# Queue positions and unit orders in a saturated spectral and SwiGLU block

## The chip, the cores and the metric

The kernel runs on one core of a Trainium2 chip. The metric is the device time of one execution in microseconds (us). The engines are TensorE (PE, with its weight loads PEld), VectorE (DVE), ScalarE (ACT), GpSimd (POOL) and SyncE (SP); each works through its own queue of instructions, and they meet through semaphores.

## The reference

One block with adaptive layer norms, all in fp32, for 2048 rows of width 512, inner width 1792:

```
mod = (silu(c) @ w_mod)            -> sa, ca, ga, sb, cb, gb
h = layernorm(x) * (1 + ca) + sa
a, b = h @ dft_hid_re.T, h @ dft_hid_im.T
x = x + ga * (dft_seq_re @ a - dft_seq_im @ b)
h = layernorm(x) * (1 + cb) + sb
x = x + gb * ((silu(h @ w1) * (h @ w3)) @ w2)
```

## The kernel before

Every fp32 operand is split into a high part, rounded to the multiplier's format (ACT, line 87, `copy`), and a low part, the rest (DVE, line 90, `minus`). A product is three matmuls: high by high, low by high, high by low. Sums of two tiles are `plus` (DVE, line 93), elementwise products `times` (DVE, line 96). Large tiles live in slots that are taken and given back in program order; the eight PSUM banks are named by number.

The first part is a layer norm and the transform along the width, until 85 us. Its products use line 576, and its last rows end in bank 5; `ho` (line 93) combines that bank with an earlier copy of it.

Then come 32 units of the transform along the sequence (`seq_unit`, line 750), until about 263 us. It accumulates eight sums, x0 to x3 and y0 to y3, in the eight banks: `x` e in bank 2e and `y` e in bank 2e + 1, so that y2 has bank 5. Each unit adds four matmuls to each x and two to each y. The first unit runs while the last rows of the transform before are still in bank 5: `between()`, the None in its order, issues those last products after x0 and x1.

The last part is the gated layer. A few plain blocks come first; then the work is twelve `items`, numbered from 0, each a group of 256 inner columns for one pair of the four tiles of 512 rows. Items 0 to 4 belong to pair 0, items 5 to 11 to pair 1; item 5 is `turning`. In an item the two large products are made from seven factors each, `a1` to `a7` for w1 and `b1` to `b7` for w3 (`factor`); each is six matmuls and accumulates in a bank that is copied out on the way (`x`, ACT line 87). The downs, `y`, multiply by w2: in items 5 to 9 again by seven factors (`seven_unit`), elsewhere directly (`down_unit`). Their results are copied out as `y` by ACT at line 335 and added to memory by a DMA that POOL issues; the last two groups' results are added by DVE instead (line 1146).

The order on PE is written out by hand as a string of units for each item, `head + body`. A minus sign marks a factor of the item before: an item's last three factors, b7, b4 and b3, run in the next item's head. A `y` takes the next of the queued downs, `seconds`.

What the other engines do for a unit is queued in program order too. `delayed()` runs at the start of each unit, and `behind(n, fn)` makes `fn` run n units later; so the number sets where an instruction stands in the queue of ACT or DVE. `result` and `seven_parts` queue the high and the low part of the gated product `hf` in this way. `beside` fills what remains of each unit with splits of weights and other background work from `jobs`: w1, w2 and w3 have a high `w1h`, a low `w1l`, and the same of their sums (`w1s`, four operations on DVE; `w1sh`, `w1sl`). `th` and `tl` are parts of the sums of the layer's input.

`judge` adds up what a check has gathered in `chk` and sets `bad`; a branch after the last down reads it.

Of the kernel before, what the change touches and what calls it, by code (L numbers as in the profile page):

```python
# [42 lines left out]
def folded(nc, pools, c, cp, wmr, wmc, x, xt, ctr, cti, wdr, wdi, w1, w3, w2, out):  # L43
# [22 lines left out]
    def give(t):  # L66
        slot, _ = slot_of.pop(id(t))
        free.append(slot)
# [657 lines left out]
    def seq_unit(n, m, between=None):  # L726
        j, k = steps[n]
        l, d, high = lo.pop((n, m)), df.pop((n, m)), bh[n][:, m, :]
        begin, turn, end = (k, m) == (0, 0), (k, m) == (NK // 2 - 1, 1), (k, m) == (NK - 1, 1)
        if begin:  # L730
            for e in range(ND):
                acc["x", e], acc["y", e] = bank(2 * e), bank(2 * e + 1)

        def own(t, e):
            return flat(t[k])[:, m * N + e * P : m * N + (e + 1) * P]

        def run(what, e):
            if what == "x":
                terms = [
                    (own(us, e), high),  # L740
                    (own(ul, e), high),
                    (own(us, e), l[:, 0, :]),
                    (own(uh, e), l[:, 1, :]),
                ]
                if k == NK // 2 and m == 1:
                    terms.append((zz[:97, 0, cols(e)], zz[:97, 1, :]))
            else:
                terms = [(own(us, e), d[:, 0, :]), (own(uh, e), d[:, 1, :])]
            for i, (lhs, rhs) in enumerate(terms):
                nc.tensor.matmul(  # L750
                    acc[what, e],
                    lhs,
                    rhs,
                    start=begin and i == 0,
                    stop=(end or (turn and what == "x")) and i == len(terms) - 1,
                    skip_group_check=what == "x" and k >= NK // 2,
                )


        order = [(what, e) for what in "xy" for e in range(ND)]  # L760
        if (k, m) == (NK // 2, 0):
            order = order[ND:] + order[:ND]
        if between:
            order = [(what, e) for e in range(ND) for what in "xy"]
            order = order[0:1] + order[2:3] + [None] + order[1:2] + order[3:]
        for at in order:
            if at is None:
                between()
            else:
                run(*at)  # L770
        give(l)
        give(d)
        if m == 1:
            give(bh.pop(n))
            if j == 1:
                for t in (uh, us, ul):
                    give(t.pop(k))

        if turn:
            for e in range(ND):  # L780
                residual(j + 2, e, acc["x", e], ga2)
        if end:
            part = [take(F32, "sum") for _ in range(2)]
            for e in range(ND):
                copy(part[e // 2][:, e % 2, :], acc["x", e])
                residual(j + 2, e, acc["y", e], ga)
            for i in range(2):
                for t in (j, j + 2):
                    step(background, 0, lambda i=i, t=t: add_sums(t, i, part[i]), 1.3)
                step(background, 0, lambda i=i: give(part[i]))  # L790
# [448 lines left out]
    def result(i, w, q, k, src):  # L1239

        g, pair = items[i]
        v = vs[i][q][:, k, :]
        if w == "w1":
            behind(k != 0 or q == 0, lambda: nc.scalar.activation(v, src, AF.Silu))  # L1244
            return
        times(v, v, src)
        if (g, pair) in SEVEN:
            seven_parts(i, q, k)
            return

        def highs():
            hf[g, PAIRS[pair][k], q] = take(F32R, "hf")
            copy(hf[g, PAIRS[pair][k], q][:, 0, :], v)

        def lows():
            u = hf[g, PAIRS[pair][k], q]
            minus(u[:, 1, :], v, u[:, 0, :].bitcast(F32))

        behind(1, highs)
        behind(2, lows)  # L1260

    def seven_parts(i, q, k):
        key = items[i]
        v = {(a, b): vs[i][a][:, b, :] for a in range(2) for b in range(2)}

        def high(n, src):
            right7[key, n] = take(F32R, "hf")
            copy(right7[key, n][:, 0, :], src)

        def low(n, src):  # L1270
            u = right7[key, n]
            minus(u[:, 1, :], src, u[:, 0, :].bitcast(F32))

        if (q, k) != (0, 1):
            n = {(0, 0): 1, (1, 0): 2, (1, 1): 3}[q, k]
            behind(1, lambda: high(n, v[q, k]))
            behind(2, lambda: low(n, v[q, k]))
            return
        t1, t2, t3, t4 = v[0, 0], v[1, 1], v[0, 1], v[1, 0]
        behind(1, lambda: minus(t1, v[0, 1], v[0, 0]))  # L1280
        behind(2, lambda: high(5, t1))
        behind(2, lambda: minus(t3, v[1, 1], v[0, 1]))
        behind(3, lambda: low(5, t1))
        behind(3, lambda: minus(t2, v[1, 1], t1))
        behind(4, lambda: high(7, t3))
        behind(4, lambda: minus(t4, v[1, 0], t2))
        behind(5, lambda: high(6, t2))
        behind(5, lambda: low(7, t3))
        behind(6, lambda: high(4, t4))
        behind(7, lambda: low(6, t2))  # L1290
        behind(8, lambda: low(4, t4))
# [69 lines left out]
    def factor(i, w, n):  # L1361
        g, pair = items[i]
        key = (w, g, pair)
        st = state.setdefault((i, w), {})
        new = n in (1, 2, 5)
        if new:
            st[TO[n]] = bank(TO[n] + (0 if w == "w1" else 3))
        to = st[TO[n]]
        names = ("h", "l") if LEFT[n][0] == "h" else ("sh", "sl")
        for d in range(2):  # L1370
            at = slice(int(LEFT[n][1]) * HALF + d * P, int(LEFT[n][1]) * HALF + (d + 1) * P)
            product(
                to,
                [flat(wuse[key][x])[:, at] for x in names],
                [x[:, d, :] for x in right(pair, n)],
                new and d == 0,
                d == 1,
                not new,
            )
        if n == 1:  # L1380
            st["x"] = take(F32, "x")
            if w == "w1":
                vs[i] = [take(F32, "v") for _ in range(2)]
        if n == 5:
            st["y"] = take(F32, "x")
        if n in (1, 5, 6):
            copy(st["y" if n == 5 else "x"][:, n // 6, :], to)
        elif n == 4:
            result(i, w, 1, 0, to)
        else:  # L1390

            own = st["y" if n == 7 else "x"][:, n % 2 if n < 7 else 0, :]
            q, k = {2: (0, 0), 3: (0, 1), 7: (1, 1)}[n]
            dst = vs[i][q][:, k, :] if w == "w1" else own
            plus(dst, to, own)
            result(i, w, q, k, dst)
            if n == 7:
                behind(1, lambda: give(st["y"]))
        st["n"] = st.get("n", 0) + 1
        if st["n"] == 7:  # L1400
            for x in wuse.pop(key).values():
                give(x)
        if n == 3:
            behind(1, lambda: give(st["x"]))
            if w == "w3":
                for x in vs.pop(i):
                    behind(9 if items[i] in SEVEN else 3, lambda x=x: give(x))


    loads.extend((n, m) for n in range(len(steps)) for m in range(2))  # L1410
# [340 lines left out]
    def unit(kind, i, n):  # L1751
# [9 lines left out]
            drain(lambda: ("t", 1, {6: 2, 5: 1, 7: 3, 4: 4}[n]) in done, jobs)  # L1761
        delayed()
        factor(i, "w1" if kind == "a" else "w3", n)
        if (kind, i, n) == ("b", turning + 1, 4):
            judge()
        if (kind, n) == ("a", 1):
            load_w(("w1", *items[i + 1]) if more else ("w2", g, pair))
        if (kind, n) == ("a", 6):
# [30 lines left out]
    for i in range(len(items)):  # L1799
        body = "a6 a5 y y a7 y a3 y a4 y b1 y b2 y b6 b5 y"  # L1800
        if i and items[i - 1] in SEVEN:
            body = "a6 a5 a7 y a3 a4 y b1 b2 y b6 b5 y"
        spread = i > 1 and items[i - 2] in SEVEN
        if spread and i < len(items) - 1:
            body = body.replace("a6", "a6 y", 1)
# [2 lines left out]
        if i == turning:  # L1808
            body = "y y y y y a6 y a5 y a7 y b1 b2 a4 b6 a3 b5"
        if i == len(items) - 1:  # L1810
            body = "a6 a5 a7 a3 a4 b1 b2 y b6 y b5 y b7 y b4 y y b3 y y y y y y y y y y"
        head = "-b7 a1 -b4 -b3 a2 " if i == turning else "-b7 a1 a2 -b4 -b3 " if i else "a1 a2 "
        if spread and i < len(items) - 1:
            head = "-b7 a1 y a2 -b4 y -b3 "
# [1 line left out]
            head = "-b7 y a1 a2 y -b4 y -b3 "  # L1816
        for at in (head + body).split():
            if at == "y":
                if (i, len(seconds)) == (len(items) - 1, 4):
                    tc.mark_branch_hint_location("general", hint="LikelyTaken")  # L1820
                down(*seconds.popleft())
            elif at[0] == "-":
                unit(at[1], i - 1, int(at[2]))
            else:
                unit(at[0], i, int(at[1]))
# [804 lines left out]
```

## Time and profile before

| | |
|---|---|
| median of 3 runs | 696.4 us (695.23 to 697.4) |
| profiled execution | 694.86 us, of which the span 693.1 us |
| PE busy in the span | 675.3 us (97%) |
| DVE, ACT, POOL busy | 586.9, 451.1, 131.6 us |
| granted PE clock | 0.997 |

Rows of the timeline give the start and duration of an instruction, or of several like ones (x2), in us, then engine, line, operation and tiles; brackets hold the idle time of the engine before it and what ended that. Rows of the waits give the total, the number of times and the longest.

### The profile page before, as it was taken

Reading aid. Unit: us, or ns where it says so; the run is one execution under the profiler, and the core shown is the slowest. Engines: PE = TensorE matmul, PEld = TensorE weight load, DVE = VectorE, ACT = ScalarE, POOL = GpSimd, SP = SyncE. Lnnn points to the kernel's source line nnn. Section 1 sums busy time; section 2 is a strip of 40 time slices with the busy share of each in tenths; the row PEclk is TensorE's granted clock in tenths of the full one; section 3 lists DMA queues with packets and bytes.
Section 4 is the critical chain, followed back from the end, with each engine's and each line's share of the span. In section 5 each row is a group of like instructions: output and inputs, shape, how many; then the busy total and the mean of one; then the engine's idle time right before and its main releaser. Section 6 shows DMA issues by size and latency. Waiting matters only on the chain.

```text
span 693.1 us, 9032 instructions
## 1 busy us (share of the span) xinstructions
PE 675.3 (97%) x3122; PEld 558.1 (81%) x3122; DVE 586.9 (85%) x945; ACT 451.1 (65%) x751; POOL 131.6 (19%) x156
## 2 busy tenths in 40 slices
PE   7999899999999999999999999999999999999996
PEld 5899778888888888888788888887877888888785
DVE  5999759998999988889997989787999979888374
ACT  4998946545353575664577767867676988877520
POOL 1320252543435000010101001011002212221100
PEclk9999999999999999999999999999999999999999
DMA  9730289787588540173667666476849898999713
GB/s 264 222 123 1 71 306 352 259 294 253 181 310 263 181 157 30 37 148 122 102 145 147 152 154 117 96 132 121 258 89 208 152 208 168 186 214 172 179 42 126
DMA packets 40261, 116.80 MB, mean 169 GB/s; under 512 B 5136, under 2 KB 5392, under 8 KB 40208
## 3 DMA queue, kind: packets, MB, share of 16 engines
q0 software_dynamic: 14512, 50.86, 36.5%
q1 hardware_dynamic: 25264, 63.98, 27.9%
q10 hardware_dynamic: 432, 1.31, 0.5%
q8 instruction: 26, 0.43, 0.3%
q14 instruction: 27, 0.22, 0.1%
HBM read 76.81 MB, written 41.42 MB: 171 GB/s over the span
## 4 chain that ended last, share of the span: by engine, by line
PE 71%; DVE 9%; issue 7%; DMA 5%; ACT 4%; POOL 1%; SPq 1%; another core or an unknown queue 1%; POOLq 0%; ACTq 0%; DVEq 0%
PE bank L100 43%; PE bank L750 25%; DMA sum<-y 3%; POOL sum L1352 1%; PE bank L559 1%; DMA w<-in_wdr 1%; PE bank L598 1%; ACT y L335 1%; DVE v L96 1%; SPq L231 1%; DMA w<-in_wdi 1%; DVE xr L805 1%; DVE ul L90 1%; DMA x<-in_x 0%
## 5 line engine op out<-in xcount | busy, mean ns | idle before, releaser
L100 PE MATMUL bank<-hf,w2h 128*128 128x512 f32 (+1 forms) x352 | 108.5, 389 | 0.4 <-ACT y L335 0.4
L87 ACT ACTIVATE hf<-v 128x512 fp32r<-128x512 f32 x71 | 44.4, 631 | 69.1 <-DVE v L96 53.7
L335 ACT ACTIVATE y<-bank,gb 128x512 f32<-128x512 f32 x118 | 76.5, 682 | 4.1 <-PE bank L100 3.6
L100 PEld LDWEIGHTS bank<-hf,w2h 128*128 128x128 f32 x352 | 65.5, 188 | 16.1 <-ACT y L335 2.2
L1160 POOL DMA_DIRECT2D sum<-y x28 | 24.0, 857 | 240.7 <-ACT y L335 124.5
L100 PE MATMUL bank<-hf,w2l 128*128 128x512 f32 (+1 forms) x176 | 68.1, 387 | 0.0
L90 DVE TENSOR_TENSOR hf<-v,hf 128x512 fp32r<-128x512 f32 x71 | 48.7, 686 | 9.8 <-ACT hf L87 9.8
L1352 POOL DMA_DIRECT2D sum<-y x35 | 29.8, 852 | 129.4 <-ACT y L335 120.4
L750 PE MATMUL bank<-d,us 128*128 128x512 f32 x128 | 49.9, 390 | 1.5 <-DVE ho L93 1.5
L87 ACT ACTIVATE x<-bank 128x512 f32<-128x512 f32 x72 | 41.7, 591 | 13.3 <-PE bank L100 12.1
L750 PE MATMUL bank<-bh,us 128*128 128x512 f32 x128 | 49.9, 390 | 0.0
L750 PE MATMUL bank<-bh,ul 128*128 128x512 f32 x128 | 49.8, 389 | 0.0
L750 PE MATMUL bank<-d,uh 128*128 128x512 f32 x128 | 49.8, 389 | 0.0
L750 PE MATMUL bank<-l,us 128*128 128x512 f32 x128 | 49.8, 389 | 0.0
L750 PE MATMUL bank<-l,uh 128*128 128x512 f32 x128 | 49.8, 389 | 0.0
L170 POOL DMA_INDIRECT re<-in_ctr,mirror x32 | 35.1, 1095 | 64.8 <-DVE ul L90 38.5
L170 POOL DMA_INDIRECT im<-in_cti,mirror x32 | 32.9, 1029 | 38.2 <-PE bank L750 10.0
L93 DVE TENSOR_TENSOR x<-bank,x 128x512 f32<-128x512 f32 x36 | 24.7, 685 | 17.3 <-PE bank L100 17.1
L100 PEld LDWEIGHTS bank<-hf,w2l 128*128 128x128 f32 x176 | 33.1, 188 | 6.6
L1244 ACT ACTIVATE v<-v 128x512 f32<-128x512 f32 x36 | 22.7, 629 | 22.5 <-DVE v L93 22.1
L93 DVE TENSOR_TENSOR v<-bank,x 128x512 f32<-128x512 f32 x36 | 24.7, 686 | 13.4 <-PE bank L100 12.5
L100 PE MATMUL bank<-h2h,w1h 128*128 128x512 f32 x80 | 31.1, 389 | 0.0
(260 smaller groups left out, 1904.7 us busy)
## 6 DMA issues: line engine op xcount, KB each, us to landing
sum<-y POOLq DMA_DIRECT2D x63, 512.0 KB
w<-in_w SPq DMA_DIRECT2D x42, 512.0 KB
re<-in_ctr SPq DMA_DIRECT2D x32, 256.0 KB
im<-in_cti SPq DMA_DIRECT2D x32, 256.0 KB
wmc<-in_wmc SPq DMA_DIRECT2D x8, 512.0 KB
xr<-in_xt SPq DMA_DIRECT2D x8, 512.0 KB
sum<-xr SPq DMA_DIRECT2D x8, 512.0 KB
x<-in_x SPq DMA_DIRECT2D x11, 256.0 KB
```

The lines of the kernel that those rows point to most:

```text
L87: nc.scalar.activation(dst, src, AF.Copy, scale=scale)
L90: nc.vector.tensor_tensor(out=dst, in0=a, in1=b, op=OP.subtract)
L93: nc.vector.tensor_tensor(out=dst, in0=a, in1=b, op=OP.add)
L96: nc.vector.tensor_tensor(out=dst, in0=a, in1=b, op=OP.mult)
L100: nc.tensor.matmul(acc, lhs[a], rhs[b], start=first and n == 0, stop=last and n == len(PASSES) - 1, skip_group_check=more,)
L170: nc.gpsimd.indirect_dma_start(dst, None, rows, bass.IndirectOffsetOnAxis(ap=at, axis=0))
L231: queue.dma_start(raw_w[dt][q * 64 : (q + 1) * 64, m, :], w[i][par::2, q])
L335: nc.scalar.activation(dst, src, AF.Identity, scale=by)
L750: nc.tensor.matmul(acc[what, e], lhs, rhs, start=begin and i == 0, stop=(end or (turn and what == "x")) and i == len(terms) - 1, skip_grou ...
L1160: nc.gpsimd.dma_start(sums[t, d // 2], y, accum_op=OP.add)
L1244: behind(k != 0 or q == 0, lambda: nc.scalar.activation(v, src, AF.Silu))
L1352: nc.gpsimd.dma_start(sums[t, which], y, accum_op=OP.add)
```

## The change

Five things move; nothing is added or taken away.

1. The first unit of the sequence transform runs y2 last, behind x3 and y3.
2. The highs of hf are queued two units behind their unit instead of one, the lows three instead of two; so are the first three parts in `seven_parts`, and v is given back one unit later outside SEVEN.
3. `judge` moves from item 6 (after b4) into the last item, ahead of the second of its last ten downs.
4. Item 6 (`turning + 1`) has its own body: downs one unit earlier, b6 behind the fourth down and b5 behind the last.
5. Item 11, the last, runs b1 and b2 among its w1 factors.

```diff
         if between:
             order = [(what, e) for e in range(ND) for what in "xy"]
-            order = order[0:1] + order[2:3] + [None] + order[1:2] + order[3:]
+            order = order[0:1] + order[2:3] + [None] + order[1:2] + order[3:5] + order[6:] + order[5:6]
...
-        behind(1, highs)
-        behind(2, lows)
+        behind(2, highs)
+        behind(3, lows)
...
-            behind(1, lambda: high(n, v[q, k]))
-            behind(2, lambda: low(n, v[q, k]))
+            behind(2, lambda: high(n, v[q, k]))
+            behind(3, lambda: low(n, v[q, k]))
...
-                    behind(9 if items[i] in SEVEN else 3, lambda x=x: give(x))
+                    behind(9 if items[i] in SEVEN else 4, lambda x=x: give(x))
...
-        if (kind, i, n) == ("b", turning + 1, 4):
-            judge()
...
             body = "a6 a5 a7 y a3 a4 y b1 b2 y b6 b5 y"
+        if i == turning + 1:
+            body = "a6 a5 y a7 a3 y a4 b1 y b2 b6 y b5"
...
-            body = "a6 a5 a7 a3 a4 b1 b2 y b6 y b5 y b7 y b4 y y b3 y y y y y y y y y y"
+            body = "a6 a5 b1 a7 a3 b2 a4 y b6 y b5 y b7 y b4 y y b3 y y y y y y y y y y"
...
             if at == "y":
+                if (i, len(seconds)) == (len(items) - 1, 9):
+                    judge()
```

Three places show what this does to the queues. On PE, in the first unit of the sequence transform, right behind x2 (bank 4). Bank 5 is y2, bank 6 x3, bank 7 y3. Before:

```order
L750 MATMUL bank4_162_1079<-l_105_720,uh_42_351 128x512
L750 MATMUL bank5_163_1080<-d_106_721,us_48_391 128x512
L750 MATMUL bank5_163_1080<-d_106_721,uh_42_351 128x512
L750 MATMUL bank6_164_1081<-bh_104_719,us_48_391 128x512
L750 MATMUL bank6_164_1081<-bh_104_719,ul_56_418 128x512
L750 MATMUL bank6_164_1081<-l_105_720,us_48_391 128x512
```

And after:

```order
L750 MATMUL bank4_162_1079<-l_105_720,uh_42_351 128x512
L750 MATMUL bank6_164_1081<-bh_104_719,us_48_391 128x512
L750 MATMUL bank6_164_1081<-bh_104_719,ul_56_418 128x512
L750 MATMUL bank6_164_1081<-l_105_720,us_48_391 128x512
L750 MATMUL bank6_164_1081<-l_105_720,uh_42_351 128x512
L750 MATMUL bank7_165_1082<-d_106_721,us_48_391 128x512
L750 MATMUL bank7_165_1082<-d_106_721,uh_42_351 128x512
L750 MATMUL bank5_163_1080<-d_106_721,us_48_391 128x512
L750 MATMUL bank5_163_1080<-d_106_721,uh_42_351 128x512
```

The two matmuls of y2 have moved behind six others.

On DVE, in the head of item 4, where the two lows of hf of item 3 are made among the splits of w3. Before:

```order
L90 TENSOR_TENSOR w3s_4089<-w_587_3914,w3s_4089 128x256
L90 TENSOR_TENSOR hf_4077<-v_3794,hf_4077 128x512
L90 TENSOR_TENSOR w3l_4106<-w_587_3914,w3h_4087 128x1024
L90 TENSOR_TENSOR hf_4095<-v_3793,hf_4095 128x512
L90 TENSOR_TENSOR w3sl_4120<-w3s_4089,w3sh_4108 128x1024
```

And after:

```order
L90 TENSOR_TENSOR w3s_4087<-w_587_3914,w3s_4087 128x256
L90 TENSOR_TENSOR w3l_4103<-w_587_3914,w3h_4085 128x1024
L90 TENSOR_TENSOR hf_4092<-v_3792,hf_4092 128x512
L90 TENSOR_TENSOR w3sl_4119<-w3s_4087,w3sh_4105 128x1024
L90 TENSOR_TENSOR hf_4108<-v_3791,hf_4108 128x512
```

Each low stands behind one more split of 1024 columns.

On ACT, in the head of item 11. Before:

```order
L87 ACTIVATE w3sh_5845<-w3s_5825 128x1024
L87 ACTIVATE x_5854<-bank_957_5847 128x512
L87 ACTIVATE hf_5866<-v_5622 128x512
L335 ACTIVATE y_5868<-bank_952_5831,gb 128x512
L335 ACTIVATE y_5868<-bank_953_5832,gb 128x512
L87 ACTIVATE x_5886<-bank_962_5879 128x512
```

And after:

```order
L87 ACTIVATE w3sh_5824<-w3s_5803 128x1024
L87 ACTIVATE x_5834<-bank_957_5827 128x512
L335 ACTIVATE y_5846<-bank_952_5810,gb 128x512
L335 ACTIVATE y_5846<-bank_953_5811,gb 128x512
L87 ACTIVATE hf_5856<-v_5600 128x512
L87 ACTIVATE x_5865<-bank_962_5858 128x512
```

The high of hf has moved behind the two copies of y.

## The prediction

> **What bounds the kernel.** I read the page first, then the waits of TensorE (PE) after the hidden transform, then the timeline of each place where PE paused.
>
> ```profile
> span 693.1 us, 9032 instructions
> PE 675.3 (97%) x3122; PEld 558.1 (81%) x3122; DVE 586.9 (85%) x945; ACT 451.1 (65%) x751; POOL 131.6 (19%) x156
> ...
> PE bank L750 <- DVE ho L93: 1.5, 1, 1.5
> PE bank L100 <- ACT y L335: 0.9, 2, 0.5
> PE bank L100 <- ACT x L87: 0.6, 2, 0.4
> ```
>
> PE is busy for 97% of the span. The last three rows are all the waits that the view names between 84 and 693 us: 3.0 us. The timeline shows somewhat more, since a pause under about 0.3 us gets no bracket and the first matmul after a pause runs slowly. So this change, which adds and removes no instruction, can only win pauses or add new ones. Where nothing waits, a unit (six matmuls) takes 1.36 us; this pair is one unit apart:
>
> ```profile
> 504.90 0.39 PE L100 MATMUL bank<-th,w1sh 128*128 128x512 f32 x1
> ...
> 506.26 0.62 PE L100 MATMUL bank<-hf,w2h 128*128 128x512 f32 x2
> ```
>
> Each place below is priced as PE's time from a first matmul to a last one, less 1.36 a unit. Gains count as minus.
>
> **First unit of the sequence transform: minus 1.36.**
>
> ```profile
> 86.46 1.12 PE L576 MATMUL bank<-wd,hh 128*128 128x256 f32 x8
> ...
> 89.03 0.39 PE L750 MATMUL bank<-l,uh 128*128 128x512 f32 x1
> 90.97 0.50 PE L750 MATMUL bank<-d,us 128*128 128x512 f32 x1 [1.55 <-DVE ho L93]
> 90.22 0.69 DVE L93 TENSOR_TENSOR ho<-bank,ho 128x512 f32<-128x512 f32 x1 [4.32 <-remote]
> ```
>
> The eight L576 products of the last rows fill bank 5, VectorE's ho empties it, and y2 needs the empty bank. Now x3 and y3 (4 + 2 matmuls, 1.36 us by the pitch above) run ahead of y2. If ho starts at 90.22 as before, y2 starts at 90.97 as before, with 1.36 of work already done: the gain is 1.36, and 0.2 of pause is left. The odd thing is that ho starts 2.6 us after the modelled end of the eight products (86.46 + 1.12 = 87.58), but only 0.8 after PE ran dry (89.03 + 0.39). If whatever released it comes only when PE runs dry, the release slides back by 1.36 too and the gain is nothing. I take the fixed time, because ho waits for the eight products alone, and keep 0 as the other end. [...]
>
> **Parts one unit later, where that helps.** The high part of hf is written by ScalarE (ACT), which works in order. A high that is queued too early waits there for VectorE and blocks the copies that free PE's banks.
>
> ```profile
> 342.61 0.63 ACT L87 ACTIVATE hf<-v 128x512 fp32r<-128x512 f32 x1 [3.74 <-DVE v L96]
> 343.15 0.67 ACT L335 ACTIVATE y<-bank,gb 128x512 f32<-128x512 f32 x1
> 343.72 1.07 ACT L87 ACTIVATE x<-bank 128x512 f32<-128x512 f32 x2
> 343.61 0.39 PE L100 MATMUL bank<-hf,w2l 128*128 128x512 f32 x1
> 344.36 0.50 PE L100 MATMUL bank<-th,w3sh 128*128 128x512 f32 x1 [0.36 <-ACT x L87]
> ```
>
> At the end of item 0, b7 should start at 343.61 + 0.23 = 343.84 and starts at 344.36: 0.52 lost, because y and x stand behind hf. Now y stands ahead of hf, during ACT's idle time, x ends at about 343.7, and b7 is on time: minus 0.52. The next wait there is x itself, 0.1 short of being late.
>
> Item 11 is the same kind, twice:
>
> ```profile
> 640.63 0.63 ACT L87 ACTIVATE hf<-v 128x512 fp32r<-128x512 f32 x1 [2.15 <-DVE v L96]
> 649.75 0.63 ACT L87 ACTIVATE hf<-v 128x512 fp32r<-128x512 f32 x1 [2.26 <-DMA sum<-y]
> 636.18 0.39 PE L100 MATMUL bank<-th,w3sh 128*128 128x512 f32 x1
> 653.79 0.39 PE L100 MATMUL bank<-th,w1h 128*128 128x512 f32 x1
> ```
>
> The two PE rows are the starts of b7 of item 10 and a4 of item 11, twelve units apart: 17.61 against 12 x 1.36 = 16.32, so 1.29 lost. Of the two ACT rows the first holds up y copies; the second waits for a slot that a DMA frees, ahead of the copy of a6 that a7 needs. Now both copies stand ahead of their hf, and b1 fills the time ahead of a7. Minus 1.29. Following ACT's new queue with the old durations, I find no copy there that PE would still wait for.
>
> **Parts one unit later, where that hurts.** The low part is VectorE's, and VectorE is in order as well. The first down of an item reads the low of the newest hf with its fifth matmul (0.91 after its start). One unit later means behind whatever weight split is queued for that unit. Item 4:
>
> ```profile
> 442.87 0.42 DVE L93 TENSOR_TENSOR w3s<-w 128x256 f32<-128x256 f32 x1
> ...
> 444.34 0.68 DVE L90 TENSOR_TENSOR hf<-v,hf 128x512 fp32r<-128x512 f32 x1
> 444.94 1.22 DVE L90 TENSOR_TENSOR w3l<-w,w3h 128x1024 fp32r<-128x1024 f32 x1
> 446.08 0.68 DVE L90 TENSOR_TENSOR hf<-v,hf 128x512 fp32r<-128x512 f32 x1
> 444.74 0.84 PE L100 MATMUL bank<-hf,w2h 128*128 128x512 f32 x2
> ```
>
> The reader is the second of the pair at 444.74, due at 444.97. Before, the low ended at 445.02, 0.05 late. Now w3l (446.08 - 444.94 = 1.14 with the overlap of neighbours) goes first: the low ends at 444.34 + 1.14 + 0.68 = 446.16, 1.19 late. Plus 1.14.
>
> Item 5 has the same shape with another split:
>
> ```profile
> 471.68 0.68 DVE L90 TENSOR_TENSOR hf<-v,hf 128x512 fp32r<-128x512 f32 x1
> ...
> 472.88 1.22 DVE L90 TENSOR_TENSOR tl<-xc,th 128x1024 fp32r<-128x1024 f32 x1
> 471.50 0.62 PE L100 MATMUL bank<-hf,w2h 128*128 128x512 f32 x2
> 479.06 0.39 PE L100 MATMUL bank<-th,w1sh 128*128 128x512 f32 x1
> ```
>
> v and tl now go first: v in hf's place at 471.68 (0.60: hf and tl stand 1.20 apart with one v between), tl (1.14 as above), then the low, ending at 471.68 + 0.60 + 1.14 + 0.68 = 474.10. It is due at 471.50 + 0.91 = 472.41: 1.69 late. But the five downs from 471.50 to 479.06 lose 7.56 - 5 x 1.36 = 0.76 to late y copies, and with PE 1.69 later those copies are in time. Plus 0.93.
>
> Items 1 to 3 have w3s (four operations) put ahead of the low:
>
> ```profile
> 384.15 0.68 DVE L90 TENSOR_TENSOR hf<-v,hf 128x512 fp32r<-128x512 f32 x1
> 384.84 0.63 PE L100 MATMUL bank<-hf,w2h 128*128 128x512 f32 x2
> DVE hf L90 <- ACT hf L87: 9.8, 14, 1.1
> ```
>
> Item 2's low ends at 384.83 and is due at 385.07: 0.24 to spare, and w3s costs 444.34 - 442.87 = 1.47. Against it, VectorE no longer waits for ACT's high just ahead (the third row: up to 1.1 each), so it comes to w3s earlier. From 0 to 1.2 an item; I take plus 0.3 for the three, near the bottom because that 1.1 returns most of the 1.47.
>
> **Items 6 and 7.** Their orders and the check's sums:
>
> ```profile
> 503.93 0.68 DVE L90 TENSOR_TENSOR hf<-v,hf 128x512 fp32r<-128x512 f32 x1
> 505.13 1.22 DVE L90 TENSOR_TENSOR w3sl<-w3s,w3sh 128x1024 fp32r<-128x1024 f32 x1
> 506.26 0.68 DVE L90 TENSOR_TENSOR v<-v,v 128x512 f32<-128x512 f32 x1
> 523.88 0.61 PE L100 MATMUL bank<-hf,w2sh 128*128 128x512 f32 x2
> 540.94 0.62 PE L100 MATMUL bank<-hf,w2sh 128*128 128x512 f32 x2
> ```
>
> From the first down of item 6 (506.26) to 523.88 stand twelve units: 17.62 - 16.32 = 1.30 lost; from there to 540.94 twelve more: 17.06 - 16.32 = 0.74. The new order moves the y copies ahead of the splits that delayed them, and I find no late copy left in item 6 when I follow ACT's new queue with the old durations: minus 1.30. But the first down now comes one unit sooner, at 504.90, and reads its newest low with the second matmul, due at 505.13; VectorE does a v and w3sl first, so that the low ends at about 503.93 + 0.60 + 1.13 + 0.68 = 506.34. Plus 1.21.
>
> ```profile
> 529.64 0.42 DVE L1015 TENSOR_REDUCE sq<-chk 128x8 f32<-128x256 f32 x1 [0.74 <-POOL sq L1014]
> ...
> 532.60 0.14 DVE L1035 TENSOR_SCALAR bad<-fine 1x1 int32<-1x1 f32 x1
> 678.48 0.75 DVE L1146 SCALAR_TENSOR_TENSOR xr<-bank,gb,xr 128x512 f32<-128x512 f32 x1 [0.61 <-PE bank L100]
> ```
>
> The check's sums hold VectorE from 529.64 to 532.74, 3.1 us, and the 0.74 of item 7 follows from it through v and ACT. They go: minus 0.74. In the last group they stand where VectorE is free for 0.61 of every 1.36 (last row). A backlog of 3.1 is worked off in 3.1 / 0.61 = 5 downs, nine are left, and five banks bridge it: 0. Were that cover gone, it would cost up to 3.1 at the very end. The small memset on GpSimd delays no DMA there, since the last group's outputs go by SyncE.
>
> **The sum.** Gains 1.36 + 0.52 + 1.29 + 1.30 + 0.74 = 5.21; losses 1.14 + 0.93 + 0.30 + 1.21 = 3.58. The net is -1.63. The profiled execution took 694.86 us (693.1 of span and 1.76 around it), which gives 693.2. The median of the runs shown is 696.4 (695.23 to 697.4), 1.5 above the profiled one; on that scale the forecast is 694.8. A measurement can tell about 0.3%, 2.1 us, from no change, so this counts as within.
>
> **Rivals.**
> First, the late lows cost about half (faster). For it: the price above supposes that every old duration and split stays where it was; a pause of PE lets VectorE catch up on what does not depend on PE. Against: strict queues leave little room, the w3l is ahead whatever happens. It gives -1.63 - 1.8 = -3.4, so 693.0. Chance 0.37.
> Second, ho's release slides with PE, the first term is 0: -0.27, so 696.1. Chance 0.08; it is within 0.3%.
> Third, slower: the low parts. The three covers seen above are -0.05, 0.24 and, in item 5, 472.41 - 472.36 = 0.05; if each first down of items 1 to 6 loses a whole unit, that is 6 x 1.36 = 8.2 instead of 3.58: -5.21 + 8.2 = +3.0, so 699.4. It decides from a total lateness of 5.21 + 2.1 = 7.3. For it: items 4 to 6 come near a unit by the rows. Against: the 1.1 of ACT wait returned at items 1 to 3. Chance 0.17.
> The sum as it stands has 0.38.
>
> **Numbers.** Faster by over 0.3%: 0.37; within: 0.38 + 0.08 = 0.46; slower: 0.17. The range goes from 692.2 (first rival, with 0.8 for the spread of the runs) to 697.8 (first term gone and 1.7 for items 1 to 3, whose upper end is 3.6). The likeliest case alone spans 693.4 to 696.2.
>
> **What would show it.** Right: no pause of PE over 0.3 us ahead of y2, b7 of item 0, item 7's first down of its own pair and a7 of item 11; new pauses of 1.2 and 1.7 us in the first downs of items 4 and 5, and of 1.2 in item 6, each released by VectorE's hf at L90. Wrong: ho starting near 91.6 instead of 90.2; no pause in items 4 to 6; or pauses of over 1 us in items 1 to 3.

## The result, and the profile after

The changed kernel takes 697.06 us (median of 14 runs, 696.01 to 699.49) against 695.85 us before (14 runs): ratio 1.0019, interval 1.0011 to 1.0027. It is slower by about 1.3 us. The profiled execution took 697.09 us, its span 695.3 us.

Two lines of the page of the changed kernel:

```profile
span 695.3 us, 9018 instructions
PE 674.3 (97%) x3122; PEld 559.0 (80%) x3122; DVE 586.9 (84%) x945; ACT 454.3 (65%) x751; POOL 132.4 (19%) x156
```

Its waits of PE from 80 us on, with the total, the number of times and the longest:

```profile
PE bank L100 <- DVE hf L90: 4.2, 4, 1.6
```

This is the whole list. All three waits named before, on ho, on y and on x, are gone from it. One has come: PE waits four times for the low part of hf, 4.2 us in all. Here are the timeline's rows at three of the four, each the low behind its split, and then PE:

```profile
443.49 1.22 DVE L90 TENSOR_TENSOR w3l<-w,w3h 128x1024 fp32r<-128x1024 f32 x1
444.62 0.69 DVE L90 TENSOR_TENSOR hf<-v,hf 128x512 fp32r<-128x512 f32 x1
445.36 0.50 PE L100 MATMUL bank<-hf,w2h 128*128 128x512 f32 x1 [1.09 <-DVE hf L90]
...
472.61 1.22 DVE L90 TENSOR_TENSOR tl<-xc,th 128x1024 fp32r<-128x1024 f32 x1
473.75 0.68 DVE L90 TENSOR_TENSOR hf<-v,hf 128x512 fp32r<-128x512 f32 x1
474.48 0.50 PE L100 MATMUL bank<-hf,w2h 128*128 128x512 f32 x1 [1.61 <-DVE hf L90]
...
506.18 1.22 DVE L90 TENSOR_TENSOR w3sl<-w3s,w3sh 128x1024 fp32r<-128x1024 f32 x1
507.32 0.68 DVE L90 TENSOR_TENSOR hf<-v,hf 128x512 fp32r<-128x512 f32 x1
508.06 0.50 PE L100 MATMUL bank<-hf,w2h 128*128 128x512 f32 x1 [1.23 <-DVE hf L90]
```

In each, the matmul starts right after the hf row ends (444.62 + 0.69 = 445.31, then 445.36). These are items 4, 5 and 6; the fourth is item 2, with 0.23 in its bracket.

PE's own stream did get shorter, though. From the first matmul of the sequence transform to the start of the last matmul it took 686.39 - 84.65 = 601.74 us before and 686.34 - 85.31 = 601.03 us after. The sequence transform began 0.66 us later in this profile (85.31 against 84.65), which is not the change's doing: in before_shift121 below, where nothing that runs was changed, it began at 85.35. The loss is behind PE. The timeline's row of VectorE's last operation, first before:

```profile
686.71 0.48 DVE L1146 SCALAR_TENSOR_TENSOR xr<-bank,gb,xr 128x256 f32<-128x256 f32 x1 [0.23 <-PE bank L100]
```

and after:

```profile
686.65 0.48 DVE L1146 SCALAR_TENSOR_TENSOR xr<-bank,gb,xr 128x256 f32<-128x256 f32 x1 [0.23 <-PE bank L100]
```

It ends at 687.19 before and at 687.13 after, and the span ends 5.9 us behind it before and 8.2 us behind it after. The records of SyncE's instructions in the trace (start in us, duration, operation, semaphore) show where that is, first before, then after:

```
688.16 0.050 COMPARE_BRANCH
690.84 0.017 EVENT_SEMAPHORE $S[100]
...
691.25 0.017 EVENT_SEMAPHORE $S[105]
691.32 0.017 EVENT_SEMAPHORE $S[106]

688.34 0.050 COMPARE_BRANCH
691.20 0.017 EVENT_SEMAPHORE $S[100]
...
691.62 0.017 EVENT_SEMAPHORE $S[105]
693.50 0.017 EVENT_SEMAPHORE $S[106]
```

SyncE closes the program with a series of semaphore operations behind its branch over the fallback. Before, they follow each other every 0.06 to 0.09 us. After, it stands still for 1.88 us between the sixth and the seventh. The view of the DMA queues from 688 us to the end shows one more load of instructions, four before:

```profile
q14 instruction: 4, 0.03, 1.4%
```

and five after (the columns are packets, megabytes and share):

```profile
q14 instruction: 5, 0.04, 1.8%
```

In the records of this queue one load runs inside the pause, from 691.76 to 692.31, and the fifth starts behind it, at 694.13. The trace does not name the engine that a load is for, so the experiments below have to show whether the pause comes from the place of the code.

The check's sums, by contrast, are hidden in the last group as forecast:

```profile
675.01 0.41 DVE L1015 TENSOR_REDUCE sq<-chk 128x8 f32<-128x256 f32 x1
...
677.96 0.14 DVE L1035 TENSOR_SCALAR bad<-fine 1x1 int32<-1x1 f32 x1
...
679.28 2.71 DVE L1146 SCALAR_TENSOR_TENSOR xr<-bank,gb,xr 128x512 f32<-128x512 f32 x4
682.51 0.75 DVE L1146 SCALAR_TENSOR_TENSOR xr<-bank,gb,xr 128x512 f32<-128x512 f32 x1 [0.52 <-PE bank L100]
```

They take 3.1 us; an addition, a low of hf and four more additions in a row follow, and at 682.51 VectorE waits for PE again.

### The profile page after: what moved, and what is told of

Same layout as the page of the kernel before. It is cut to its first block, busy times and chain, and to the rows that moved or that the text cites. A ratio compares the mean times of both kernels' runs of the same rounds, so it can differ in the third digit from the quotient of the medians.

```text
span 695.3 us, 9018 instructions
## 1 busy us (share of the span) xinstructions
PE 674.3 (97%) x3122; PEld 559.0 (80%) x3122; DVE 586.9 (84%) x945; ACT 454.3 (65%) x751; POOL 132.4 (19%) x156
## 4 chain that ended last, share of the span: by engine, by line
PE 85%; DVE 8%; ACT 3%; issue 1%; DMA 1%; another core or an unknown queue 1%; SPq 0%; DVEq 0%; ACTq 0%
PE bank L100 56%; PE bank L750 25%; PE bank L559 2%; PE bank L598 1%; ACT hm L501 1%; DVE v L96 1%; PE bank L576 1%; DMA x<-in_x 1%; DVE x L93 1%; DVE st L449 1%; DVE ul L90 1%; DVE hf L90 1%; DVE v L93 0%; DVE hl L90 0%
```

## The experiments

The compiled programs give the theory its numbers. Ahead of SyncE's closing code stand 593 instructions before the change and 586 after: reordered work needs fewer semaphore instructions, four fewer in the kernel, and three fewer in the fallback, which is compiled behind it. The traces show the four (SyncE executed 351 instructions before, 166 of them semaphore operations, and 347 with 162 after); the fallback does not run and is in no trace. The theory assumes that code comes in blocks, which no trace shows; seven instructions are then enough if a block now ends among the closing operations. "End of the code as before" below means that unused loads in the fallback bring the number back to 593.

| kernel | ratio to before, interval | PE's stream, us | from VectorE's last operation to the end, us | SyncE instructions ahead |
|---|---|---|---|---|
| before (its profile) | 1 | 601.74 | 5.9 | 593 |
| after | 1.0019 (1.0011 to 1.0027) | 601.03 | 8.2 | 586 |
| after_shift7 | 0.9995 (0.9986 to 1.0005) | 600.63 | 6.0 | 593 |
| before_shift121 | 1.0040 (1.0027 to 1.0053) | 601.43 | 8.1 | 714 = 586 + 128 |
| first_unit_only | 0.9983 (0.9970 to 0.9997) | 600.34 | 6.0 | 593 |
| judge_only | 0.9992 (0.9978 to 1.0006) | 599.92 | 6.5 | 593 |
| parts_only | 1.0017 (1.0008 to 1.0026) | 602.95 | 6.0 | 593 |
| low_before_split | 0.9931 (0.9914 to 0.9948) | 597.24 | 6.1 | 593 |
| low_before_split_again | 0.9949 (0.9934 to 0.9963) | 597.20 | 6.2 | 593 |
| lows_with_highs | 0.9943 (0.9930 to 0.9956) | 597.50 | 6.4 | 593 |
| lows_mixed | 0.9945 (0.9926 to 0.9964) | 596.71 | 5.9 | 593 |
| low_before_split_shift20 | 0.9956 (0.9939 to 0.9973) | 596.68 | 6.2 | 613 |

**after_shift7.** In the fallback alone:

```diff
     nc.sync.dma_start(cc, cp)
+    spare = consts.tile([1, 7], F32, name="spare")
+    for n in range(7):
+        nc.sync.dma_start(spare[:, n : n + 1], c[:, n : n + 1])
```

> The changed kernel, with seven small loads more on SyncE's queue in the fallback code that never runs, so that the code behind it lies seven instructions further, where it lay before the change. Theory 1 (the end of the program waits for instruction code on SyncE because the change shortened its code by seven instructions): the pause of 1.9 us among SyncE's closing semaphores goes, all else stays; the span ends 5.9 to 6.3 us after VectorE's last operation instead of 8.2, about 1.9 us under the changed kernel and 0.3 to 1.0 us under the kernel before (ratio 0.9985 to 0.9995). Theory 2 (the check's sums at the end, or the last transfers, hold up the end): the late end stays, ratio 1.002.

Measured: 695.17 us, ratio 0.9995. PE's four waits for hf are the same 4.2 us; the pause in SyncE's series is gone and the end is 6.0 us behind VectorE. Nothing that runs was changed, so the 1.9 us was the place of the code. (PE's stream is 0.4 us shorter than the changed kernel's all the same: ho came sooner here, see the last section.)

**before_shift121.** The same edit on the kernel before, with 121 loads.

> The kernel before with 121 small loads more in the fallback code that never runs, so that on SyncE the code behind it lies, in blocks of 128 instructions, where it lies in the changed kernel. Theory 1 (the end waits for a block of code): a pause of about 1.9 us appears among SyncE's closing semaphores, plus 1.5 to 2.3 us, ratio 1.002 to 1.0035. Theory 2 (the length of the code does not matter): 1.000.

Measured: 698.01 us, ratio 1.0040. The pause appears between the same two semaphore operations (691.91 to 693.94), and the same additional load of instructions in the view of the DMA queues:

```profile
q14 instruction: 5, 0.04, 1.9%
```

So the code before carries the loss as well once it is put there. A shift by 128, from 586 to 714, leaves the pause at the same place. A block of 128 was the author's estimate: the loads of that queue from 688 us on are 8192 bytes each before and in the changed kernel, and how many instructions one holds is not shown. The ratio is somewhat more than the pause alone, 2.8 us (1.9 to 3.7) against 2.0.

**first_unit_only.** The edit to `order` in `seq_unit` alone.

> The kernel before with y2 last in the first unit and nothing else. If ho's release keeps its time: minus 1.3 us (ratio 0.998), ho starting as long after the eight last-row products as before (2.6 us after their modelled end). If the release slides with TensorE: no change (1.000), ho starting 0.8 us after TensorE has run dry.

Measured: 694.17 us, ratio 0.9983. The timeline's rows of y2 on PE and of ho on VectorE:

```profile
90.82 0.50 PE L750 MATMUL bank<-d,us 128*128 128x512 f32 x1 [0.30 <-DVE ho L93]
90.08 0.69 DVE L93 TENSOR_TENSOR ho<-bank,ho 128x512 f32<-128x512 f32 x1 [4.43 <-PE bank L750]
```

ho starts at 90.08, as it did before (90.22), with six matmuls more queued in front of y2. Its release does not slide with PE, and 0.30 of wait is left of 1.55. PE's stream is 1.4 us shorter.

**judge_only.** The two edits around `judge` alone.

> The kernel before with the check's sums moved into the last group and nothing else; the code keeps its length on SyncE. Theory 1: the pause of 0.7 us ahead of item 7's first down goes and the end stays 6 us behind VectorE's last operation: minus 0.7 (ratio 0.999). Theory 2 (the sums hold up the end): plus 1.3 or more (1.002).

Measured: 694.49 us, ratio 0.9992, with an interval that reaches 1.0006. The timing alone does not tell 0.7 us from nothing; the profile does: no pause ahead of item 7's first down is left, and the end is 6.5 us behind VectorE's last operation. The sums do not hold up the end. PE's stream is 1.8 us shorter, but only 0.7 of that is item 7; another 0.7 is y2's wait for ho, 0.83 instead of 1.55, though nothing was changed there.

**parts_only.** The five edits to `behind` alone, with ten unused loads.

> The kernel before with highs and lows one unit later and nothing else; end of the code as before. Late lows cost 0.5, 1.4 and 1.1 us at items 2, 4 and 5 (its y copies included), none at item 6, whose first down is a unit later here; gains 0.8 at items 0 and 1, 1.2 at item 11 and up to 1.1 at item 6; the 0.7 of item 7 stays. Sum between 0 and plus 1.0 us, ratio 1.000 to 1.0015. If the low parts were no cost: minus 2 to 3 us, 0.996 to 0.997.

Measured: 696.53 us, ratio 1.0017 (1.0008 to 1.0026): just above the range expected, whose upper end was 1.0015. The waits of PE from 90 us on:

```profile
PE bank L100 <- DVE hf L90: 2.9, 3, 1.6
PE bank L750 <- DVE ho L93: 1.5, 1, 1.5
PE bank L100 <- ACT y L335: 0.5, 1, 0.5
PE bank L100 <- ACT x L87: 0.4, 1, 0.4
```

The lows of items 2, 4 and 5 cost 2.9 us in brackets. Two of the expectations failed. The pauses at item 6 stay, so they needed the new body. The pause ahead of item 7's first down is gone, so two parts of the change take away the same pause (one of 0.34 comes at b7 of item 7). That of item 11 is gone as expected, so the new body was not needed there.

**low_before_split, twice.** The low leaves its place behind the weight splits and nothing else: it is queued within its second unit, behind the sums of that unit and ahead of `beside`.

```diff
+    mids = []
+
+    def settle():
+        while mids:
+            mids.pop(0)()
...
-        behind(3, lows)
+        behind(2, lambda: mids.append(lows))
...
         factor(i, "w1" if kind == "a" else "w3", n)
+        settle()
```

The low of `seven_parts` is edited likewise, `down` calls `settle` as well, and four unused loads keep the end of the code where it was.

> The changed kernel with the low parts queued at the end of their second unit, behind its sums and ahead of its weight splits, instead of at the start of the third; code length set so that the end lies as before the change. If the late lows are what the change lost (theory 1): the pauses of items 2, 4 and 6 go to under 0.2 us, that of item 5 from 1.9 to about 0.6, and with all gains kept it comes out 4.5 to 5.5 us under the kernel before (ratio 0.992 to 0.994). If the lows only show up as the last of several waits (theory 2), the pauses stay over 1 us with another releaser, ratio 0.998.

> The same kernel as low_before_split once more, since one of its six runs took the fallback branch (3877 us) and left few runs. If that was a rare event that has nothing to do with the queues: all runs near 691 us, ratio 0.992 to 0.994. If the late check is at fault, more runs of that length.

Measured: 691.19 and 691.16 us, ratios 0.9931 and 0.9949. One of the first six runs took 3877 us, by its length the fallback; none of the second six did, nor any of the nine of low_before_split_shift20, which executes the same. Why stays open; the ratios leave that run out. PE's only wait from 90 us on:

```profile
PE bank L100 <- DVE hf L90: 0.5, 1, 0.5
```

and its row in the timeline, at item 5:

```profile
471.85 0.50 PE L100 MATMUL bank<-hf,w2h 128*128 128x512 f32 x1 [0.48 <-DVE hf L90]
```

With the slow start of the first matmul behind a pause (0.34 us to the next start instead of 0.23, at 471.85 above), item 2 loses nothing, item 4 the 0.23 that it lost before the change too, item 6 0.37 and item 5 0.75. PE's stream is 3.8 us shorter than the changed kernel's. The late lows were real, and they were the only large loss in PE's stream.

**lows_with_highs.** `behind(2, lows)` and `behind(2, lambda: low(...))`, at the start of the second unit, with v given back one unit earlier again (3 instead of 4) and five unused loads.

> The changed kernel with the lows back at their second unit, at its start, right behind the highs; end of the code as before the change. If only the place of the low against the weight splits counts: like low_before_split or up to 0.5 us better, since item 5's low now also stands ahead of the sums of its unit (ratio 0.992 to 0.994, no pause over 0.2 us at items 2, 4, 5 and 6). If VectorE, in order, now waits for ScalarE's high of the same unit and passes that wait on: pauses of 0.3 to 0.7 us come back at several items, ratio 0.995 to 0.998.

Measured: 691.5 us, ratio 0.9943, no bracket in PE's waits from 90 us on. Both expectations were half right: item 5's low is in time, and pauses of about 0.35 us come at the first downs of items 7 and 10 and at b7 of item 7. PE's stream is no shorter.

**lows_mixed.** `behind(2, lows)` in `result`, `mids` in `seven_parts`, and four unused loads.

> The changed kernel with the lows of the pair-0 items and of item 10 on at the start of their second unit, as in lows_with_highs, and those of the seven-factor items at its end, as in low_before_split; end of the code as before the change. If the pauses of the two kernels belong to their own items: no pause over 0.2 us at items 4 and 5 and 0.4 us less than low_before_split at item 5 (its 0.75 goes, up to 0.4 of late y copies comes back), none at item 7; 0 to 0.5 us under low_before_split, ratio to the kernel before 0.993 to 0.9945. If they belong to VectorE's queue as a whole, no better than either.

Measured: 690.59 us, ratio 0.9945; beside it on the same chip low_before_split_shift20 took 691.19. The intervals don't tell them apart, and neither does PE's stream, 596.71 us here and 596.68 there. Each expectation holds in part: item 5 loses 0.4 us less than in low_before_split and item 7 nothing, but 0.2 come back at items 1 to 3 and 0.1 at the end. The largest pause left is 0.36 us, at item 6. It beats the kernel before by 3.8 us (2.5 to 5.1), and so the changed kernel too, which was slower than before, though the two did not run side by side.

**low_before_split_shift20.**

> low_before_split with its end twenty instructions further on SyncE's queue. If only the block boundary among the closing instructions costs: no pause there, and the same time as low_before_split within 0.5 us. If the end is only right at the one place where it lay before: about 1.9 us more.

Measured: 691.19 us, ratio 0.9956, no pause in SyncE's series. With 613 instructions ahead the end is as good as with 593 (6.2 against 6.1 us); of the four places tried, only 586 and 714 have the pause.

## Why the prediction was wrong

It forecast 1.6 us less, and 1.3 us more was measured. The sign fell on a term that was not in it. That the measured 697.06 us lies in the range of 692.2 to 697.8 is luck: its upper end stood for a release of ho that slides and for 1.7 us more at items 1 to 3, and neither came.

**The step that failed** is the one that says that the change adds and removes no instruction, and with it the sum, whose only terms are PE's pauses and which gives the end a cost of 0. The work is the same (PE, VectorE, ScalarE and GpSimd have the counts of before), but the semaphore instructions are not: 9032 instructions became 9018 by the first line of the page, four of the 14 on SyncE. With the three in the fallback, which the page does not count, SyncE's closing code moved by seven places, to one that has the pause. That is 2.3 us in the profile (8.2 - 5.9), of which the pause is 1.88, and 1.7 us by the medians of the changed kernel with and without the shift, each against its own runs of before: 0.0019 + 0.0005 of 696. The check's sums, which the prediction looked at for the end, were hidden. The 1.76 us around the span held (697.09 - 695.3 = 1.79).

**PE's stream**: forecast -1.63, measured -0.71 (601.03 - 601.74). Each stretch below is PE's time less 0.2267 a matmul (1.36 / 6), between the same places of the stream before and after (rounded; the differences add up to -0.71):

| place | forecast | measured (before to after) |
|---|---|---|
| y2 | -1.36 | -1.43 (1.94 to 0.51) |
| b7 of item 0 | -0.52 | -0.57 (0.65 to 0.08) |
| items 1 to 3 | +0.30 | +0.49 (0.27 to 0.76) |
| item 4 | +1.14 | +1.15 (0.24 to 1.40) |
| item 5 | +0.93 | +1.23 (0.76 to 1.99) |
| item 6, gains | -1.30 | -1.29 (1.29 to 0) |
| item 6, low | +1.21 | +1.50 (0.04 to 1.54) |
| item 7 | -0.74 | -0.71 (0.71 to 0) |
| behind it, to item 10 | 0 | +0.21 (0.03 to 0.23) |
| item 11 and its head | -1.29 | -1.29 (1.29 to 0) |

Every place and every sign that was forecast was right, and the releaser was VectorE's hf in all four waits. The lows were under-sized, by 0.2 at items 1 to 3 and by 0.3 each at items 5 and 6: I priced how late the operand is, while PE also pays for the time from the low's end to its own start (0.05, 445.31 to 445.36) and for a slow first matmul after it (0.34 to the next start instead of 0.23). Item 4 comes out right because PE had paid these before the change as well: the low that was 0.05 late cost it 0.24. The gains had been measured as whole pauses and held these costs already. With the 2.3 us at the end the profiles make 1.6 us more, against 1.3 (0.8 to 1.9) by the runs.

**The rivals.** The first (lows at half the price) is out: full price and more. The second (ho's release slides) is out: ho started at 90.08 in first_unit_only. The third had the right sign with the wrong mechanism: the pauses at the lows come to about 5.5 us in all (0.50 and 0.23 at items 2 and 3, 1.36, 1.89 and 1.50 at items 4 to 6), short of the 7.3 from which it would decide. Without the code's place, after_shift7 has 0.9995, 0.3 us less than before, with an interval from -1.0 to +0.3.

**The term of y2** took the release of ho at a fixed time, and that held: 90.08 in first_unit_only against 90.22 before, with six more matmuls ahead of y2. Why ho starts 2.6 us behind its products is not shown: see below.

## What to carry to other kernels

In a kernel whose main engine is 97% busy, a number that moves work by one unit moves it past whatever is queued there: write down, for each queue, what is now ahead of it, and who reads it first. Here the high part wanted to be later, and the low part did not; they were tied together only by habit. And compare the number of instructions on each engine as well as the work: here a gain of 0.71 us in PE's stream was lost to a pause of 1.88 us, which came with seven instructions fewer ahead of SyncE's closing code.

## What was not expected of the hardware

The place of code at the end of a program: 1.88 us (691.62 to 693.50) in the changed kernel and 2.03 us (691.91 to 693.94) in before_shift121, both times behind the sixth of SyncE's closing operations (586 + 6 = 592 and 714 + 6 = 720 instructions, 128 apart), and none at 593 and 613. The closing operations follow SyncE's branch, and the first of them starts 2.68 us behind it before (688.16 to 690.84) and 2.86 us behind it in the changed kernel (688.34 to 691.20); what fills that time is not shown. The same pause at positions 128 apart agrees with the author's estimate of a block of 128 instructions. That the pause is a wait for such a block is a reading that fits all four positions; no record names what SyncE waits for.

The release of ho: in ten of the twelve profiles it started 1.75 to 2.75 us after the modelled end of the eight products that it waits for, whether PE had run dry or not (90.22 before, 90.08 in first_unit_only). In lows_mixed it came at once:

```profile
87.68 1.11 PE L576 MATMUL bank<-wd,hh 128*128 128x256 f32 x8
88.83 0.69 DVE L93 TENSOR_TENSOR ho<-bank,ho 128x512 f32<-128x512 f32 x1 [1.73 <-PE bank L576]
```

87.68 + 1.11 = 88.79, and ho starts at 88.83. The same holds in low_before_split_shift20, on the same chip. The semaphore that ho waits for shows where the time goes: PE raises it after the fourth and after the eighth product, and in lows_mixed it rises at 88.33 and 88.81, 0.015 us behind their modelled ends; before, it rises at 90.14 and 90.20, while the modelled ends are 87.10 and 87.58. By these records VectorE is not late; both of PE's signals are. What holds them back stays open; the runs only show that it is not PE's later work.
